# A fused attention and ELU network kernel: two plain token blocks in place of three, with all sums of weights made in the second block

## The chip, the cores and the metric

The kernel runs on one core of one Trainium2 chip. The metric is the device time of one execution in microseconds (us); lower is better. Several executions are timed and their median is used. One more execution is taken with the hardware profiler, and the profile describes that one. Five engines work side by side, each on its own queue of instructions in order: TensorE (PE, with its weight loads as PEld), VectorE (DVE), ScalarE (ACT), GpSimd (POOL), and SyncE (SP), which here issues every DMA.

## The reference

Attention runs within chunks of 64 tokens, for 8 batches of 576 tokens, 8 heads of 64 values. Its output, 4608 tokens of 512 values, goes through a two-layer network with an ELU between the layers. All arithmetic is to float32 accuracy.

```
scores = scale * matmul(q_c, k_c^T)            # q, k, v cut into chunks of 64 tokens
attn = exp(scores - max) ; attn = attn / (sum(attn) + 1e-09)
x = matmul(attn, v_c) -> [4608, 512]
h = x @ w_in                                   # w_in [512, 2048]
g = where(h > 0, h, exp(min(h, 0)) - 1)
out = g @ w_out                                # w_out [2048, 512]
```

## The kernel before

**Accuracy by parts.** TensorE multiplies in a format with fewer bits than float32 (F32R). Each operand is therefore split into a high part (`hi`, a rounded copy made on ACT) and a low part (`lo`, the difference, made on DVE or POOL), and each product is three matmuls: hi·hi, hi·lo and lo·hi (`three`, L427).

**Blocks.** The 4608 tokens are 9 blocks (`NB`) of 512 (`TB`). The 2048 hidden columns are 16 groups (`NF`) of 128, written f. A block is four tiles (`tt`) of 128 tokens; tile n of attention is made one block ahead of its use, in about ten small steps that a generator hands out (`later_attention`, L347). The steps that matter here are: two DVE transposes of q and k (L358), the score matmuls (L364), maximum and subtraction (L371, L372), exponent (L376), the sum, its reciprocal and the multiplication (L379 to L387), eight small DMAs `y<-y` that move the quarters (L396), a DVE transpose to `turned` (L398), the matmuls with v (L405), and the copy to `xf` (L410).

**Plain blocks.** The first `PLAIN` = 3 blocks take each f in turn: `hidden(f)` is 12 matmuls of 512 columns into PSUM, `elu` is two ACT steps, a DVE step (L450), the high part on ACT (L455) and the low part on DVE (L458), and `project(f)` is again 12 matmuls, one f later. The strings `FIRST_BLOCK`, `SECOND_BLOCK`, `LATER` and `LAST_STEPS` write out the order within an f: `H` is `hidden`, each `e` one step of `elu`, `P` the projection, `a` a step of the tile in work, `n` a step of the one after it.

**Blocks by seven products.** The other six blocks take two f at a time (a pair). The first layer of a pair is a 2 by 2 block product made with seven products instead of eight (a Winograd form), each 6 matmuls of 256 columns. These use sums and differences of the weight blocks: S1, S2, S3, S4, beside A11, A12, A22. They also use sums of the tokens' blocks: T1 to T4, beside B11, B21, B22, made by `prepare_x` (L581) with `x` items. `PAIRS`, `FIRST_PAIR`, `OPENING_PAIR` and `LAST_PAIR` write out the order: `p1` to `p7` are products, `c` and `d` take their results from PSUM on ACT (L632) and DVE (L637), `A` and `B` are steps of the two ELU halves, `Q` is three matmuls of 512 columns of the second layer, `w` loads a quarter of a pair's weights, `L` loads the next tile's q and k.

**Sums of weights.** `combine` (L501) makes the sums for the eight pairs g once. For each g, POOL adds high and low parts (two wide additions) and forms S1, S2, S4, S3 (four narrow ones) into one of two of the three staging buffers `kept_st`. `split(g)` cuts the sums into high and low parts, on ACT (L533) and DVE (L534). `write_parts` and `write_sums` write everything to a scratch tensor in DRAM (`a_dram`) with six DMAs (L528, L529, L539). The sums of the pair after next can start only when the writes from the same buffer have landed. One step of `combine` is issued after each f of blocks 1 and 2, three steps for each g, 27 in all. `load_operands` (L556) then reads `a_dram` back, four DMAs of 448 KB for a pair, into memory that held the plain weights.

**Tokens.** `load_tokens` (L236) reads q and k of a tile, 4 DMAs each; where a tile straddles two batches (n = 4, 13, 22, 31) it takes 8 each. Tiles up to 9 use the staging buffers 2 and 1 in turn, and later ones buffer 0, or 0 and 1.

**Queues.** PE, ACT, DVE and SP run in the order in which the program issues (`manual_schedule`). An instruction that waits holds all behind it on its engine. On SP a DMA that waits for its data holds every later DMA.

Of the kernel before, what the change touches and what calls it, by code (L numbers as in the profile page):

```python
# [10 lines left out]
F32 = mybir.dt.float32  # L11
# [4 lines left out]
ALU = mybir.AluOpType  # L16
# [4 lines left out]
def kernel(  # L21
# [35 lines left out]
    PLAIN = 3  # L57
# [289 lines left out]
    def later_attention(tt: int, qk, v_sb):  # L347
# [30 lines left out]
        z = sm.tile([P, 2, NK, 2], F32, name="z")[:, :, :, :1]  # L378
        nc.vector.tensor_reduce(out=z, in_=scores, axis=AX.X, op=ALU.add)  # L379
        nc.vector.tensor_scalar_add(z, z, 1e-9)  # L380
        nc.vector.reciprocal(z, z)
# [87 lines left out]
    def store(blk: int, o_ps, tts):  # L469
        for tt in tts:  # L470
# [6 lines left out]
            (nc.vector.tensor_copy if tt % 2 else nc.scalar.copy)(out=o, in_=o_ps[tt])  # L477
# [23 lines left out]
    def combine():  # L501
# [5 lines left out]
        def place_of(g):  # L507
            return kept_st[1 + g % 2][:, :2 * 8 * P].rearrange("p (l a f) -> p l a f", l=2, f=P)
# [33 lines left out]
        for step in range(3 * NG + 3):  # L542
            for g in range(NG):
                since = step - 3 * g - 2 + (g % 4 == 3)
                if since == 0:
                    sums(g)
                if since == 1:
                    write_parts(g, 0)
                if since == 2:
                    split(g)  # L550
                    write_parts(g, 1)
                if since == 3:
                    write_sums(g)
            yield
# [26 lines left out]
    def prepare_x(pool, tag):  # L581
# [10 lines left out]
        def part(name):  # L592
            if name in sources:
                hi, lo = b_operand(name)
                nc.scalar.copy(out=hi, in_=sources[name])
                nc.gpsimd.tensor_tensor(  # L596
# [74 lines left out]
    def warm(n: int):  # L671
# [48 lines left out]

    PAIRS = (
        "p1 c1 x1 Q p2 d1 w B Q p6 c2 B Q B x2 p5 w x3 n n Q p7 c3 d2 A w a Q Q p4 c4 A w Q p3 d3 "
        "A A Q B",
        "n a a L p1 c1 Q p2 d1 w B Q p6 c2 B Q B n n p5 w Q n p7 c3 d2 A w n l Q Q p4 c4 A w Q p3 d3 "
# [5 lines left out]
        "n a a L p1 c1 xB11 Q p2 d1 w B Q p6 c2 B Q B xB21 n p5 w xt1b n xt2b Q p7 c3 xT2 d2 A "  # L730
        "n n l Q Q p4 c4 A w Q p3 d3 A A xt4b xt3b xT1 Q w"
    )
    OPENING_PAIR = (
        "p1 c1 B Q p2 d1 xT3 B w Q p6 B c2 B Q n p5 xT4 w Q p7 c3 d2 xB22 A n w a Q Q p4 c4 A w "
# [6 lines left out]
    )  # L741
    FIRST_PAIR = (
        "Q Q Q p1 c1 xT1 xt3b Q p2 d1 xT3 Q p6 c2 xT4 w n n Q p5 xB22 w Q p7 c3 d2 w Q a A p4 c4 w "
        "p3 A d3 A A B"
# [86 lines left out]
    def place_of_tokens(n: int):  # L831

        if n < 2 * NTT + 2:
            return kept_st[2 - n % 2]
# [177 lines left out]
```

## Time and profile before

| | |
|---|---|
| timed executions | 862.87, 866.29, 864.86 us, median 864.86 us |
| the profiled execution's own time | 865.55 us |
| its span, first to last instruction | 863.8 us |
| mean granted TensorE clock | 0.996 |
| busy: ACT, DVE, POOL | 56%, 59%, 25% of the span |
| DMA moved | 180.47 MB, mean 209 GB/s |

The profile gives for each group of instructions a source line, the engine, the tile written and those read, the count, the busy time and the mean duration, and what ended the idle time before them. The chain of work that ended last goes back from the last instruction to whatever released it. The timeline lists instructions by start time, in us from the start of the span. Block 1 begins at about 134 us, block 2 at 229 us, the first pair at 320 us, and each later block is 90 us long.

### The profile page before, as it was taken

The numbers are of one execution on the slowest core, as the hardware profiler recorded it, in microseconds if no ns is written. First come the engines' busy times: TensorE is split into PE (matmuls) and PEld (weight loads), VectorE is DVE, ScalarE is ACT, GpSimd is POOL, SyncE is SP. The second block draws the span as 40 slices with busy tenths as digits, with TensorE's granted clock in tenths as the row PEclk, the third lists the DMA queues.
The fourth block names the chain that finished last, engine by engine and source line by source line (L and its number), as shares of the span: only waits on it lengthen the run. The fifth ranks groups of instructions, "written<-read, shape, count | busy, mean of one in ns | idle before, by whom it ended". The sixth has DMA issues, their size and how long they took to land.

```text
span 863.8 us, 17307 instructions
## 1 busy us (share of the span) xinstructions
PE 848.0 (98%) x6622; PEld 731.1 (85%) x6622; DVE 512.2 (59%) x841; ACT 483.7 (56%) x931; POOL 219.2 (25%) x185
## 2 busy tenths in 40 slices
PE   7899999999999999999999999999999999999998
PEld 6688887788888888888888888888888898889897
DVE  5899886556756566456644674458456854542222
ACT  5799985344544346455644565456554654465443
POOL 2000003126233023223422342234222522252221
PEclk9899999999999999999999999999999999999999
DMA  8886552546477758887778968886868798557521
GB/s 189 212 269 182 196 136 72 159 124 211 147 222 224 224 171 245 262 247 215 223 245 263 282 206 258 261 257 202 273 209 262 212 286 263 205 191 241 171 87 49
DMA packets 156707, 180.47 MB, mean 209 GB/s; under 512 B 67024, under 2 KB 123344, under 8 KB 156624
## 3 DMA queue, kind: packets, MB, share of 16 engines
q1 hardware_dynamic: 156624, 179.36, 68.0%
q8 instruction: 52, 0.85, 0.4%
q14 instruction: 31, 0.25, 0.1%
HBM read 147.85 MB, written 24.12 MB: 199 GB/s over the span
## 4 chain that ended last, share of the span: by engine, by line
PE 91%; SPq 3%; DMA 3%; DVE 2%; POOL 0%; ACT 0%; issue 0%; DVEq 0%
PE o L430 44%; PE h L430 42%; PE ps_a L364 2%; PE ps_a L405 2%; SPq L219 1%; SPq L230 1%; DMA wi_hi<-a_dram 1%; DMA k_sb<-in_k_dram 1%; DMA st<-in_moe_w_out_dram 1%; DMA y<-y 1%; PE ps_a L297 0%; PE ps_a L313 0%; SPq L396 0%; DVE glo L458 0%; PE ps_a L266 0%
## 5 line engine op out<-in xcount | busy, mean ns | idle before, releaser
L653 POOL TENSOR_TENSOR wi_lo<-e,wi_hi 128x512 fp32r<-128x512 f32 x84 | 108.6, 1293 | 325.3 <-ACT wi_hi L649 325.3
L430 PE MATMUL h<-xhi,wi_hi 128*128 128x256 f32 (+1 forms) x704 | 189.5, 315 | 0.4 <-DVE kept L637 0.3
L637 DVE TENSOR_TENSOR kept<-h,kept 128x256 f32<-128x256 f32 x144 | 60.8, 422 | 173.4 <-PE h L430 110.9
L632 ACT COPY kept<-h 128x256 f32<-128x256 f32 x192 | 70.2, 366 | 161.5 <-PE h L430 161.5
L430 PE MATMUL o<-wo_lo,wi_hi 128*128 128x512 f32 x384 | 152.3, 397 | 0.0
L430 PE MATMUL o<-wo_hi,wi_hi 128*128 128x512 f32 x384 | 152.0, 396 | 0.0
L430 PE MATMUL o<-wo_hi,wi_lo 128*128 128x512 f32 x384 | 149.4, 389 | 0.0
L430 PE MATMUL h<-xlo,wi_hi 128*128 128x256 f32 (+1 forms) x448 | 147.0, 328 | 0.1
L430 PEld LDWEIGHTS h<-xhi,wi_hi 128*128 128x128 f32 x704 | 123.4, 188 | 16.4 <-DVE kept L637 1.3
L430 PE MATMUL h<-xhi,wi_lo 128*128 128x256 f32 (+1 forms) x448 | 131.4, 330 | 0.0
L430 PEld LDWEIGHTS h<-xlo,wi_hi 128*128 128x128 f32 x448 | 84.2, 188 | 12.1 <-POOL xlo L596 0.3
L430 PEld LDWEIGHTS h<-wi_lo,wi_hi 128*128 128x128 f32 x576 | 81.6, 189 | 9.4 <-ACT kept L632 1.2
L430 PEld LDWEIGHTS h<-xhi,wi_lo 128*128 128x128 f32 x448 | 79.7, 188 | 11.2 <-DVE kept L637 0.4
L644 DVE SCALAR_TENSOR_TENSOR e<-e,kept 128x512 f32<-128x512 f32 x96 | 67.2, 700 | 34.7 <-ACT e L642 19.0
L430 PEld LDWEIGHTS o<-wo_hi,wi_lo 128*128 128x128 f32 x384 | 72.2, 188 | 16.1
L430 PE MATMUL h<-wi_lo,wi_hi 128*128 128x256 f32 x576 | 84.7, 283 | 0.0
L649 ACT CAST wi_hi<-e 128x512 fp32r<-128x512 f32 x96 | 59.8, 623 | 36.2 <-DVE e L644 35.9
L641 ACT ACTIVATE e<-kept 128x512 f32<-128x512 f32 x96 | 60.6, 632 | 34.1 <-DVE kept L637 33.7
L430 PE MATMUL o<-wo_hi,ghi 128*128 128x512 f32 x192 | 76.3, 397 | 0.0
L505 POOL TENSOR_TENSOR kept<-wi_hi,wi_lo 128x512 f32<-128x512 f32 x16 | 20.8, 1322 | 215.7 <-DVE qT L358 136.7
L430 PEld LDWEIGHTS o<-wo_lo,wi_hi 128*128 128x128 f32 x384 | 73.5, 191 | 2.3
L430 PE MATMUL o<-wo_hi,glo 128*128 128x512 f32 x192 | 74.9, 390 | 0.3 <-DVE glo L458 0.3
(98 smaller groups left out, 1382.9 us busy)
## 6 DMA issues: line engine op xcount, KB each, us to landing
wi_hi<-a_dram SPq DMA_DIRECT2D x128, 448.0 KB, 5.7
wi_lo<-a_dram SPq DMA_DIRECT2D x64, 448.0 KB, 5.7
kept<-in_q_dram SPq DMA_DIRECT2D x100, 128.0 KB, 7.4
kept<-in_k_dram SPq DMA_DIRECT2D x100, 128.0 KB, 4.4
st<-in_moe_w_in_dram SPq DMA_DIRECT2D x16, 512.0 KB, 4.2
st<-in_moe_w_out_dram SPq DMA_DIRECT2D x16, 512.0 KB, 4.8
a_dram<-kept SPq DMA_DIRECT2D x16, 512.0 KB, 4.4
y<-y SPq DMA_DIRECT2D x224, 32.0 KB, 1.9
```

The lines of the kernel that those rows point to most:

```text
L219: nc.sync.dma_start(out=dst[p0:p0 + n], in_=src[b, :, s0:s0 + n, :].rearrange("h s d -> s h d"))
L230: nc.sync.dma_start(out=v_sb[j * C:(j + 1) * C, :, c, :], in_=v[b, j::2, ss, :].rearrange("h s d -> s h d"),)
L364: nc.tensor.matmul(scores[halves[c], j, hp, :], lhsT=qT[halves[j], hp, halves[c]], rhs=kT[halves[j], hp, halves[c]], start=True, stop=True,)
L405: nc.tensor.matmul(x_ps[halves[j], c, hp, :], lhsT=v_sb[halves[c], 2 * hp + j, :], rhs=turned[halves[c], j * NK + hp, :], start=True, stop ...
L430: nc.tensor.matmul(ps, lhsT=a, rhs=b, start=start, stop=stop, skip_group_check=onto)
L505: nc.gpsimd.tensor_tensor(out=out, in0=a, in1=b, op=op)
L632: nc.scalar.copy(out=out, in_=self.x)
L637: nc.vector.tensor_tensor(out=out, in0=self.y, in1=self.kept[kept], op=ALU.add)
L641: nc.scalar.activation(out=e, in_=c, func=AF.Relu, scale=-1.0)
L644: nc.vector.scalar_tensor_tensor(out=e, in0=e, scalar=-1.0, in1=c, op0=ALU.add, op1=ALU.max)
L649: nc.scalar.copy(out=ghi, in_=e)
L653: engine.tensor_tensor(out=glo, in0=e, in1=ghi.bitcast(F32), op=ALU.subtract)
```

## The change

- `PLAIN` is 2: block 2 is now done by seven products, and block 1 is the last plain block.
- `combine` runs within block 1, in 17 steps: one at its start and one after each f. For pair g the POOL sums are issued at step `begin[g]`, and the split and all six writes at `end[g]` (the last pair's writes one step later). The two staging buffers are now 2 and 1 instead of 1 and 2.
- Tiles from 9 on use buffer 0, and odd ones above 12 buffer 2. The pair stage keeps its own results in buffer 1 instead of 2.
- In block 1, `plain_loads` issues two quarters after each of f = 9, 10, 11 and two after f = 15; before, it was 1, 2, 1 after f = 9, 10, 11 and 2, 2 after 13, 14.
- The last three plain steps and the first pair are reordered: the transposes of the following tile come one f earlier, some token sums come later, the last two ELU steps of f = 15 move behind product p2 of the first pair, products p2 and p6 follow closely, and the low part of B22 is made on DVE (`yB22`).
- In all pairs, `L` moves from the head of each second pair to the later part of each first pair. In the last pair of a block, `xt4b` moves from behind `d3` to before it.
- In attention the sum and its increment `z` are in a free part of the PSUM bank instead of SBUF; the reciprocal still goes to SBUF.
- The four results of block 0 are copied out of PSUM on ACT alone; before, two on ACT and two on DVE.

```diff
-    PLAIN = 3
+    PLAIN = 2
...
-        z = sm.tile([P, 2, NK, 2], F32, name="z")[:, :, :, :1]
-        nc.vector.tensor_reduce(out=z, in_=scores, axis=AX.X, op=ALU.add)
-        nc.vector.tensor_scalar_add(z, z, 1e-9)
-        nc.vector.reciprocal(z, z)
+        z = sm.tile([P, 2, NK, 1], F32, name="z")
+        z_ps = banks[0][:, :, NK * C:NK * C + NK].rearrange("p j (h e) -> p j h e", e=1)
+        nc.vector.tensor_reduce(out=z_ps, in_=scores, axis=AX.X, op=ALU.add)
+        nc.vector.tensor_scalar_add(z_ps, z_ps, 1e-9)
+        nc.vector.reciprocal(z, z_ps)
...
-            (nc.vector.tensor_copy if tt % 2 else nc.scalar.copy)(out=o, in_=o_ps[tt])
+            (nc.vector.tensor_copy if tt % 2 and blk else nc.scalar.copy)(out=o, in_=o_ps[tt])
...
-            return kept_st[1 + g % 2][:, :2 * 8 * P].rearrange("p (l a f) -> p l a f", l=2, f=P)
+            return kept_st[2 - g % 2][:, :2 * 8 * P].rearrange("p (l a f) -> p l a f", l=2, f=P)
...
-        for step in range(3 * NG + 3):
+        begin, end = (0, 1, 2, 4, 5, 6, 8, 9), (2, 4, 5, 6, 8, 9, 10, 12)
+        for step in range(NF + 1):
             for g in range(NG):
-                since = step - 3 * g - 2 + (g % 4 == 3)
-                if since == 0:
+                if step == end[g]:
+                    split(g)
+
+                if step == (end[g] if g < NG - 1 else end[g] + 1):
+                    write_parts(g, 0)
+                    write_parts(g, 1)
+                    write_sums(g)
+                if step == begin[g]:
                     sums(g)
-                if since == 1:
-                    write_parts(g, 0)
-                if since == 2:
-                    split(g)
-                    write_parts(g, 1)
-                if since == 3:
-                    write_sums(g)
             yield
...
     PAIRS = (
-        "p1 c1 x1 Q p2 d1 w B Q p6 c2 B Q B x2 p5 w x3 n n Q p7 c3 d2 A w a Q Q p4 c4 A w Q p3 d3 "
+        "p1 c1 x1 Q p2 d1 w B Q p6 c2 B Q B x2 p5 w x3 n n Q p7 c3 d2 A w a Q Q L p4 c4 A w Q p3 d3 "
         "A A Q B",
-        "n a a L p1 c1 Q p2 d1 w B Q p6 c2 B Q B n n p5 w Q n p7 c3 d2 A w n l Q Q p4 c4 A w Q p3 d3 "
+        "n a a p1 c1 Q p2 d1 w B Q p6 c2 B Q B n n p5 w Q n p7 c3 d2 A w n l Q Q p4 c4 A w Q p3 d3 "
         "A A Q B w",
     )
...
     LAST_PAIR = (
-        "n a a L p1 c1 xB11 Q p2 d1 w B Q p6 c2 B Q B xB21 n p5 w xt1b n xt2b Q p7 c3 xT2 d2 A "
-        "n n l Q Q p4 c4 A w Q p3 d3 A A xt4b xt3b xT1 Q w"
+        "n a a p1 c1 xB11 Q p2 d1 w B Q p6 c2 B Q B xB21 n p5 w xt1b n xt2b Q p7 c3 xT2 d2 A "
+        "n n l Q Q p4 c4 A xt4b w Q p3 d3 A A xt3b xT1 Q w"
     )
     OPENING_PAIR = (
-        "p1 c1 B Q p2 d1 xT3 B w Q p6 B c2 B Q n p5 xT4 w Q p7 c3 d2 xB22 A n w a Q Q p4 c4 A w "
+        "p1 c1 B Q p2 d1 xT3 B w Q p6 B c2 B Q n p5 xT4 w Q p7 c3 d2 xB22 A n w a Q Q L p4 c4 A w "
         "Q p3 d3 A A Q B"
     )
     LAST_STEPS = (
-        "H e e e e a xt1a xt2a xt4a xt3a P",
-        "n n H e e e P n a a e n",
-        "H xB11 n xt1b xB21 e n xt2b e n xT2 e e xt4b R",
+        "H e e e e n n a xt1a xt2a xt4a xt3a P",
+        "H e e e P n a a e xt1b xt2b",
+        "H n xB11 xB21 n e xT2 n e n R",
     )
     FIRST_PAIR = (
-        "Q Q Q p1 c1 xT1 xt3b Q p2 d1 xT3 Q p6 c2 xT4 w n n Q p5 xB22 w Q p7 c3 d2 w Q a A p4 c4 w "
-        "p3 A d3 A A B"
+        "Q Q Q p1 c1 Q p2 e e d1 xt3b xT1 p6 xT3 c2 Q xt4b Q w p5 n n xT4 yB22 Q p7 c3 d2 w Q a A p4 c4 w "
+        "p3 A d3 A A w L B"
     )
...
-        for _ in range({LOADED + 1: 1, LOADED + 2: 2, LOADED + 3: 1, NF - 3: 2, NF - 2: 2}.get(f, 0)):
+        for _ in range({LOADED + 1: 2, LOADED + 2: 2, LOADED + 3: 2, NF - 1: 2}.get(f, 0)):
             next(loading)
...
-        if n < 2 * NTT + 2:
-            return kept_st[2 - n % 2]
-        return kept_st[1 if n % 2 and n > (PLAIN + 1) * NTT else 0]
+        if n == 2 * NTT:
+            return kept_st[2]
+        return kept_st[2 if n % 2 and n > (PLAIN + 1) * NTT else 0]
...
+            if (blk, f) == (PLAIN - 1, 0):
+                next(combining)
...
-                if blk > 0:
-                    next(combining, None)
                 if blk == PLAIN - 1:
+                    next(combining)
                     plain_loads(f)
```

More of the change, by code (lines that the diff above doesn't have):

```diff
@@ L590, in prepare_x, with part @@
                        "t3": (t3, b22, b12)}
-        def part(name):
+        def part(name, engine=nc.gpsimd):
             if name in sources:
@@ L595, in part @@
                 nc.scalar.copy(out=hi, in_=sources[name])
-                nc.gpsimd.tensor_tensor(
+                engine.tensor_tensor(
                     out=lo, in0=sources[name], in1=hi.bitcast(F32), op=ALU.subtract)
@@ L883 @@
                                             for _ in range(3)][::-1]
-                                sums = kept_st[2]
+                                sums = kept_st[1]
                                 loaded = later_loads(2 * NTT)
@@ L943 @@
                         pair.add(int(item[1]))
+                    elif item == "e":
+                        acts[blk - 1, NF - 1] = next(act)
                     elif item == "A":
@@ L961 @@
                         next(following, None)
+                    elif item[0] == "y":
+                        preparing(item[1:], nc.vector)
                     elif item[0] == "x":
```

## The prediction

> **What bounds the kernel now.** The page comes first: who is busy, and for what share of the span.
>
> ```profile
> PE 848.0 (98%) x6622; PEld 731.1 (85%) x6622; DVE 512.2 (59%) x841; ACT 483.7 (56%) x931; POOL 219.2 (25%) x185
> ```
>
> PE is the bound; the others matter only where PE waits for them. The view of stretches says the same for each stage (columns: stretch, its length, busy time and count of PE, PEld, DVE, ACT, POOL, then granted clock, DMA share, GB/s).
>
> ```profile
> 153.70:246.00 92.30, 92.30 (x641) 75.80 (x641) 56.60 (x84) 42.19 (x68) 24.99 (x25) 1.00 0.55 167
> 506.77:596.77 90.00, 89.98 (x785) 79.72 (x785) 53.35 (x93) 48.95 (x97) 27.38 (x22) 1.00 0.81 248
> ```
>
> The clock is granted in full, so a stage costs its matmuls plus the waits. The chain in order of time gives periods: the same matmul, one or four tiles later.
>
> ```profile
> 172.98 2.72 PE o L430 x12
> 176.79 2.95 PE h L430 x12
> 269.11 2.95 PE h L430 x12
> 397.87 0.91 PE h L430 x6
> 420.75 0.91 PE h L430 x6
> 602.07 0.91 PE h L430 x6
> 624.44 0.91 PE h L430 x6
> ```
>
> A plain block takes 269.11 - 176.79 = 92.32 us. Within a block by seven products a tile takes 624.44 - 602.07 = 22.37 us, and across a block's end 420.75 - 397.87 = 22.88 us: each boundary holds a wait of 0.51 us, and a block takes 3 x 22.37 + 22.88 = 89.99 us. Last, the timeline of PE shows the other waits after block 0.
>
> ```profile
> 152.98 0.69 PE L405 MATMUL ps_a<-turned,v_sb 64*64 64x64 f32 x32 [0.93 <-DVE turned L398]
> ...
> 322.22 0.40 PE L430 MATMUL o<-wo_hi,ghi 128*128 128x512 f32 x1
> 322.45 0.40 PE L430 MATMUL o<-wo_lo,ghi 128*128 128x512 f32 x1
> 323.17 0.50 PE L430 MATMUL o<-wo_hi,glo 128*128 128x512 f32 x1 [0.32 <-DVE glo L458]
> ...
> 325.36 0.35 PE L430 MATMUL h<-xhi,wi_hi 128*128 128x256 f32 x1 [0.29 <-DVE kept L637]
> ...
> 443.51 0.69 PE L405 MATMUL ps_a<-turned,v_sb 64*64 64x64 f32 x32 [0.85 <-DVE turned L398]
> ```
>
> Undisturbed, one follows the last in 0.23 us (322.22 to 322.45), so from 322.45 to 323.17 PE lost 0.49, which is the bracket's 0.32 and 0.17 for the restart. With the same restart the wait at 325.36 lost 0.46, and with a smaller one at 329 us the transition to the first pair loses about 1.2 us. The two waits for `turned` lost 1.1 and 1.0 us. All that can be won beside the block itself is thus 1.1 + 1.2 + 1.0 + 5 x 0.51 = 5.9 us.
>
> **The change part by part.**
>
> *One block more by seven products:* 89.99 - 92.32 = **-2.3 us**. It also adds a sixth boundary, which is in the 89.99.
>
> *Boundaries.* DVE is what is late there:
>
> ```profile
> 406.57 1.09 DVE L380 TENSOR_SCALAR z<-z 128x8 f32<-128x8 f32 x1
> 410.59 1.54 DVE L601 TENSOR_TENSOR t<-xf,t 128x256 f32<-128x256 f32 x1
> 412.05 0.41 DVE L601 TENSOR_TENSOR t<-xf 128x256 f32<-128x256 f32 x1
> 412.38 0.41 DVE L637 TENSOR_TENSOR kept<-h,kept 128x256 f32<-128x256 f32 x1
> 185.26 0.17 DVE L380 TENSOR_SCALAR z<-z 128x8 f32<-128x8 f32 x1
> ```
>
> `d1` of the new block (412.38) ends at 412.79, and PE waits for it. Ahead of it stand the increment of z, 1.09 us where it takes 0.17 elsewhere, and two token sums of 1.54 and 0.41 (0.41 seems to be the undisturbed price). With z in PSUM and `xt4b` ahead of `d3`, up to 0.9 + 1.1 us leave this queue, and 0.17 to 0.5 are needed. But `d3` itself moves behind `xt4b`, and p2 of the next block needs it. Bounds: 0 to -0.51 for each of six boundaries; I take half: **-1.5 us**.
>
> [...]
>
> *`L` earlier.* The wait at 443.51 comes from SP:
>
> ```profile
> 420.70 7.68 SPq L247 DMA_DIRECT2D kept<-in_q_dram  x8
> 434.81 6.57 SPq L396 DMA_DIRECT2D y<-y  x8
> ```
>
> Tile 22 straddles two batches, and its 16 DMAs hold SP from 420.70 on for most of the time until 434.81, where `y<-y` comes. `L` now stands two products and some Q earlier (3 to 4 us), so `y<-y` can go some 4 us sooner, against 1.0 us needed: **-1.0 us** (0 to -1.0). In tiles with 8 DMAs nothing was late, so nothing is won.
>
> *The first wait (153 us).* ACT takes two copies from DVE, which stood between the subtraction and the sum of tile 8:
>
> ```profile
> 142.19 1.28 DVE L477 COPY q_sb<-o 128x512 f32<-128x512 f32 x2
> ```
>
> Most of the 1.28 us lay beside the exponent on ACT, on which the sum waits too. I take a quarter for `y<-y` and the PE wait behind it: **-0.3 us** (0 to -1.1).
>
> *All sums in block 1.* POOL's work is the same, in half the time; the issue is the order on ACT and DVE. `split(3)` is issued after f = 5, directly ahead of the transposes of tile 10, whose scores PE wants at 175.63; `split(6)` stands likewise ahead of tile 11, wanted at 198.71.
>
> ```profile
> 158.81 0.62 ACT L455 CAST ghi<-e 128x512 fp32r<-128x512 f32 x1 [0.75 <-DVE e L450]
> 168.55 0.98 SPq L539 DMA_DIRECT2D a_dram<-kept  x2
> 172.46 2.56 POOL L505 TENSOR_TENSOR kept<-wi_hi,wi_lo 128x512 f32<-128x512 f32 x2 [18.54 <-DMA a_dram<-kept]
> 175.10 3.38 POOL L505 TENSOR_TENSOR kept<-kept 128x256 f32<-128x256 f32 x4
> L533 ACT CAST kept<-kept 128x1024 fp32r<-128x1024 f32 x8 | 8.4, 1048 | 0.0
> L534 DVE TENSOR_TENSOR kept<-kept 128x1024 fp32r<-128x1024 f32 x8 | 11.3, 1416 | 1.2 <-ACT kept L533 1.1
> 172.38 1.08 DVE L358 STREAM_TRANSPOSE k_apart<-kept 128x512 f32<-128x512 f32 x1
> 175.63 0.69 PE L364 MATMUL ps_a<-k_apart,qT 64*64 64x64 f32 x32
> 183.40 1.22 DVE L534 TENSOR_TENSOR kept<-kept 128x1024 fp32r<-128x1024 f32 x1 [0.26 <-ACT kept L533]
> 198.71 0.69 PE L364 MATMUL ps_a<-k_apart,qT 64*64 64x64 f32 x32
> ```
>
> On the clock of the profile before: f = 3 leaves ACT at 159.43; split(1) takes ACT to 160.5 and DVE to 161.9; two writes are issued by 163.0; they land 2.9 us later, as at 169.53 to 172.46; POOL works 6.0 us (172.46 to 178.48) and ends sums(3) at 171.9; split(3) takes ACT to 173.0, DVE to 174.4, and the two transposes (1.08 each, a little overlapped: 2.0) to 176.4. With 0.1 us for the hand-over PE waits 0.9 us. From split(4), which ends where 183.40 + 1.22 stood, the same sum for tile 11 gives 199.2, a wait of 0.5 us. All that is queued behind on DVE, the ELU of f = 6 and 10, has a projection's time (2.72 us, the row at 172.98) before PE asks for it. In both places DVE's low parts and splits now run beside POOL, each up to one POOL instruction (1.3 us) later; I add 0.55 each: **+2.5 us**. Bounds: 0 if POOL ends 1 us sooner, and +8 if POOL costs 1.3 and the writes land 2.8 us later than at 172.46.
>
> The other splits stand in front of work with slack. On SP the six writes (3 us) stand ahead of `y<-y` in three tiles, whose `turned` came 4 us before its use in block 2.
>
> *The transition.* In the new order p2 and p6 follow closely, the last ELU has 1.4 us more, and `d1` is done before p5; the waits of 0.49 and 0.46 go. New: p6 needs T2's low part, made by POOL after the high part (about 0.4 us late), and p3 needs B22's low part and `d2`, which now stand behind transposes and copies (0.6 us; both are estimates from the durations shown: two transposes 2.0, a copy of 0.64). Then two quarters of the second pair's weights are issued only after f = 15, behind eight `y<-y`:
>
> ```profile
> 321.49 4.95 SPq L396 DMA_DIRECT2D y<-y  x8
> 331.36 0.39 PE L430 MATMUL h<-xhi,wi_lo 128*128 128x256 f32 x1
> wi_hi<-a_dram SPq DMA_DIRECT2D x128, 448.0 KB, 5.7
> ```
>
> With the multiplications 0.7 us later, they are issued at 327.2 and land at 332.9 by the median, 1.7 us after the second pair's first product; one that lands as soon as the writes above (3.9 us after its issue, 168.55 to 172.46) would be in time. I take 0.5. Together -1.2 + 1.0 + 0.5 = **+0.3 us** (-1.2 to +3).
>
> *Nothing:* the PLAIN tests, buffers and stores. Buffer 1 must be written out before the first pair's `c1`; that is 10 us earlier. Block 0 and the last block are unchanged.
>
> Sum: -2.3 - 1.5 - 1.0 - 0.3 + 2.5 + 0.3 = **-2.3 us** on the profiled execution's 865.55 us (span 863.8), thus 863.3. That execution lies 0.7 us above the median of 864.86; on the median's scale: **862.6 us**. A measurement of this kernel tells about 0.5%, 4.3 us, from no change: the forecast is "within".
>
> **The rivals.**
>
> *The sums hide.* If POOL ends a microsecond sooner, the +2.5 goes: -4.8. If the boundaries too give their whole 3.1 us and the transition its 1.2, it is -7.9. For it: POOL is busy only 25.0 of 92.3 us in block 1 now, and the waits found are below 1 us. Against it: two separate chains must both gain. Time: 857 to 860. Chance 0.29.
>
> *The writes land late* (slower). All of `a_dram` is written within some 70 us; the q1 traffic of block 1 rises from 167 GB/s by about half of 14.7 MB and eight loads of 448 KB, 11 MB in 92 us, to some 285 GB/s, above the 248 of the stage with a DMA share of 0.81. Each microsecond of late landing after 172.46's 2.9 moves tile 10, tile 11 and the second pair's load: 3 us for one. From 2.2 us on (a landing of 5.1 us) the time is over 4.3 us above the old one; at 3 us it is 871.6. Against it: SP issues a pair's writes in bursts with pauses of 6 us and more. Chance 0.08.
>
> *The reorderings reach nothing:* boundaries, `y<-y` and transition stay as they are, only the block and the new waits count: -2.3 + 2.5, 865. The increment of z and `xt4b` speak against it; that both wait for POOL's instructions, whose times also move, speaks for it. Chance 0.13.
>
> *POOL in the way:* low part and split, in both chains, each wait as long as the sum at 410.59 (1.54 against 0.41, 1.1 us): 4.5 us in place of my 1.1, so 866.0. For it: POOL is then busy 8 x 6.0 of 92 us in block 1. Against it: in both chains the split itself comes when the next sums still wait for their buffer. Chance 0.10. [...]
>
> **How the numbers follow.** Forecast 0.40, reorderings reach nothing 0.13, POOL in the way 0.10, sums hide 0.29, late writes 0.08. Faster by over 0.5% (below 860.5): 0.29. Within: 0.40 + 0.13 + 0.10 = 0.63. Slower: 0.08. The range from 858.5 to 866.5 leaves out the late writes and the lower third of the hidden sums.
>
> **What would show it.** Right: the period of a late block falls from 89.99 towards 89.5; no wait for `turned` near tile 21; in block 1 waits of 0.5 to 2 us at L364 for DVE's transposes, in tiles 10 and 11, with ACT's split waiting for POOL. Wrong: waits of several us in block 1 or none at all; POOL's sums held by landings of 5 us; a wait at the second pair's p1 for a load. A whole block's cost other than 90 us would upset the first term.

## The result, and the profile after

The changed kernel takes 870.2 us (median of 8 executions, 866.67 to 872.56) against 865.73 us of the kernel before on the same chip (8 executions): a ratio of 1.0055, 95% interval 1.0041 to 1.0069. On a second chip it was 869.82 against 864.01 us, 1.0070 (1.0057 to 1.0082). The forecast was 862.6 us, range 858.5 to 866.5: the kernel is slower by a little over the 0.5% that can be told, and outside the range. The profiled execution after took 869.94 us (span 868.2, mean clock 0.994), 4.4 us more than the one before.

The page's first part, of the changed kernel (lines are one to three higher than before, L364 is the same):

```profile
PE 844.5 (97%) x6766; PEld 736.4 (85%) x6766; DVE 513.8 (59%) x854; ACT 496.5 (57%) x968; POOL 245.9 (28%) x205
```

PE works 3.5 us less than before and the kernel takes 4.4 us more: the time went into waits. The timeline of PE after the first block shows them, the idle time and its releaser in brackets.

```profile
135.86 0.50 PE L431 MATMUL h<-xlo,wi_hi 128*128 128x512 f32 x1 [0.80 <-DVE xlo L424]
...
177.98 0.69 PE L364 MATMUL ps_a<-k_apart,qT 64*64 64x64 f32 x32 [1.75 <-DVE k_apart L358]
...
202.57 0.69 PE L364 MATMUL ps_a<-k_apart,qT 64*64 64x64 f32 x32 [1.45 <-DVE k_apart L358]
...
243.92 0.73 PE L406 MATMUL ps_a<-turned,v_sb 64*64 64x64 f32 x32 [2.13 <-DVE turned L399]
...
245.96 0.79 PE L431 MATMUL h<-xhi,wi_lo 128*128 128x256 f32 x2 [0.59 <-DMA wi_lo<-a_dram]
...
449.65 0.56 PE L406 MATMUL ps_a<-turned,v_sb 64*64 64x64 f32 x22 [1.13 <-DVE turned L399]
```

The waits of before at 153 us (`turned` of tile 8) and at each block's end are gone. New are one at the seam of blocks 0 and 1, the two foreseen ones for the scores of tiles 10 and 11, and a long one at the transition to the first pair, where 2.13 us for `turned` of tile 12 is followed by 0.59 us for the second pair's weights. The view of stretches (columns as in the prediction) shows that the transition cost more than these waits:

```profile
240.00:243.00 3.00, 1.79 (x41) 1.46 (x40) 0.73 (x2) 1.52 (x3) 0.00 (x0) 1.00 0.44 60
243.00:246.00 3.00, 1.50 (x35) 1.10 (x35) 1.62 (x3) 1.50 (x3) 0.84 (x1) 0.74 0.83 234
246.00:249.00 3.00, 3.00 (x12) 2.90 (x13) 0.45 (x2) 1.12 (x3) 0.43 (x1) 0.50 1.01 392
249.00:252.00 3.00, 3.00 (x14) 2.62 (x14) 1.87 (x3) 0.95 (x3) 0.00 (x0) 0.62 1.05 418
252.00:255.00 3.00, 3.00 (x21) 2.65 (x20) 1.64 (x5) 0.85 (x3) 1.30 (x1) 1.00 1.06 342
...
255.22:344.72 89.50, 89.50 (x786) 79.83 (x785) 52.83 (x93) 48.84 (x98) 27.38 (x21) 1.00 0.82 245
```

From 244 to 252 us the granted clock is 0.50 to 0.74: PE is busy, and does 12 and 14 matmuls in 3 us where it does 21 afterwards. The last row is the good part: the first block by seven products takes 89.50 us with PE busy all through.

What made `turned` late stands on SP's queue and on DVE (each row the start, the time of issue, and the count):

```profile
215.83 5.06 SPq L397 DMA_DIRECT2D y<-y  x8
...
225.01 5.38 SPq L247 DMA_DIRECT2D kept<-in_q_dram  x8
230.43 3.70 SPq L247 DMA_DIRECT2D kept<-in_k_dram  x8
234.23 1.36 SPq L219 DMA_DIRECT2D v_sb<-in_v_dram  x2
235.69 5.02 SPq L397 DMA_DIRECT2D y<-y  x8
240.75 1.68 SPq L566 DMA_DIRECT2D wi_lo<-a_dram  x2
```

```profile
212.66 0.76 DVE L388 TENSOR_TENSOR y<-ps_a,z 128x256 f32<-128x256 f32 x2
...
232.72 0.74 DVE L388 TENSOR_TENSOR y<-ps_a,z 128x256 f32<-128x256 f32 x2
...
243.15 0.71 DVE L399 STREAM_TRANSPOSE turned<-y 128x512 f32<-128x512 f32 x1 [2.42 <-DMA y<-y]
```

The data of `y<-y` is ready at 233.46 (232.72 + 0.74), but SP is still issuing the 16 token DMAs of tile 13 and the loads of v, and begins `y<-y` at 235.69, 2.2 us later. PE's wait is 2.1 us. The two quarter loads of the second pair come behind it. SP was as late one tile earlier: the data of tile 11 is ready at 213.42 (212.66 + 0.76), and its `y<-y` starts at 215.83, 2.4 us later. Between the starts of the two `y<-y` SP has 19.9 us of work, with gaps of 0.1 us at most, and the two data times are 20.0 us apart, so it cannot catch up.

The seam's wait is one that the prediction did not have. POOL forms the second pair's sums already in block 0, because its staging buffer is no longer used by tile 9:

```profile
131.97 3.28 POOL L507 TENSOR_TENSOR kept<-kept 128x256 f32<-128x256 f32 x4
...
134.59 1.22 DVE L424 TENSOR_TENSOR xlo<-xf,xhi 128x512 fp32r<-128x512 f32 x1
```

Beside it the last `glo` of block 0 took 1.15 us on DVE and the first `xlo` 1.22 us, where in the kernel before `glo` took 0.69 us and the four `xlo` took 2.49 together (start to end, one on the heels of the other):

```profile
133.41 2.49 DVE L423 TENSOR_TENSOR xlo<-xf,xhi 128x512 fp32r<-128x512 f32 x4
```

Put together, with 0.17 us for each restart of PE as in the prediction, from the two profiled executions:

| step | predicted, us | measured, us | from |
|---|---|---|---|
| start to block 1 (unchanged code) | 0 | +0.7 | the same matmul at 134.68 and 133.96 |
| seam of blocks 0 and 1 | not seen | +1.0 | 0.80 + 0.17 |
| first wait | -0.3 | -1.1 | gone |
| tiles 10 and 11 | +2.5 | +3.5 | 1.75 + 1.45 + 2 x 0.17 |
| transition | +0.3 | +5.4 | what is left of 4.4; worked out below |
| `L` earlier | -1.0 | +0.3 | 1.13 for 0.85 |
| block in place of a plain one, with its boundary | -2.3 | -2.8 | 89.50 - 92.32 |
| the five boundaries there were | -1.5 (with the sixth) | -2.5 | 5 x 0.51 gone |
| sum (of the unrounded values) | -2.3 | +4.4 | |

The transition by itself: 2.13 and 0.59 with their restarts, 0.7 us of small waits at 234 and 238 us, and (from an experiment below) some 2.6 us of the lowered clock make 6.4 us; the remainder gives 5.4 + the 1.2 of before = 6.6.

### The profile page after: what moved, and what is told of

It is laid out like the page before. It is cut to its first block, busy times and chain, and to the rows that moved or that the text cites. A ratio compares the mean times of both kernels' runs of the same rounds, so it can differ in the third digit from the quotient of the medians.

```text
span 868.2 us, 17806 instructions
## 1 busy us (share of the span) xinstructions
PE 844.5 (97%) x6766; PEld 736.4 (85%) x6766; DVE 513.8 (59%) x854; ACT 496.5 (57%) x968; POOL 245.9 (28%) x205
## 4 chain that ended last, share of the span: by engine, by line
PE 86%; DMA 4%; SPq 4%; DVE 2%; POOL 1%; ACT 1%; issue 1%; DVEq 0%; POOLq 0%; ACTq 0%
PE o L431 42%; PE h L431 39%; PE ps_a L364 2%; POOL kept L507 1%; PE ps_a L406 1%; DMA wi_lo<-a_dram 1%; SPq L219 1%; SPq L397 1%; SPq L230 1%; DMA k_sb<-in_k_dram 1%; DMA st<-in_moe_w_out_dram 1%; DMA a_dram<-kept 1%; PE ps_a L313 0%; DMA y<-y 0%; DVE kept L536 0%
## 5 line engine op out<-in xcount | busy, mean ns | idle before, releaser
L655 POOL TENSOR_TENSOR wi_lo<-e,wi_hi 128x512 fp32r<-128x512 f32 x98 | 126.6, 1292 | 387.2 <-ACT wi_hi L651 387.2
L431 PE MATMUL o<-wo_lo,wi_hi 128*128 128x512 f32 x448 | 178.0, 397 | 0.0
L431 PE MATMUL o<-wo_hi,wi_hi 128*128 128x512 f32 x448 | 177.7, 397 | 0.0
L431 PE MATMUL o<-wo_hi,wi_lo 128*128 128x512 f32 x448 | 174.5, 390 | 0.0
L431 PE MATMUL h<-xlo,wi_hi 128*128 128x256 f32 (+1 forms) x424 | 133.8, 316 | 0.8 <-DVE xlo L424 0.8
L431 PE MATMUL h<-xhi,wi_lo 128*128 128x256 f32 (+1 forms) x432 | 118.8, 319 | 0.6 <-DMA wi_lo<-a_dram 0.6
L431 PEld LDWEIGHTS h<-wi_lo,wi_hi 128*128 128x128 f32 x666 | 94.4, 189 | 10.4 <-POOL wi_lo L598 0.8
L431 PE MATMUL h<-wi_lo,wi_hi 128*128 128x256 f32 x666 | 97.7, 282 | 0.2 <-POOL wi_lo L598 0.2
L431 PEld LDWEIGHTS o<-wo_hi,wi_hi 128*128 128x128 f32 x448 | 84.8, 189 | 3.0
L644 ACT ACTIVATE e<-e 128x512 f32<-128x512 f32 x112 | 70.8, 632 | 3.6
```

The costliest lines, as they stand in the source:

```text
L431: nc.tensor.matmul(ps, lhsT=a, rhs=b, start=start, stop=stop, skip_group_check=onto)
L644: nc.scalar.activation(out=e, in_=e, func=AF.Exp, scale=-1.0)
L655: engine.tensor_tensor(out=glo, in0=e, in1=ghi.bitcast(F32), op=ALU.subtract)
```

## The experiments

**Is it SP's queue?** The theory: SP has more to issue in block 1 than it has time for, so `y<-y` waits its turn. The first test takes work from SP in block 1: the writes of the weights' own parts, 4 DMAs a pair, move into block 0. Their bytes move with them.

```diff
             for g in range(NG):
+                if step == 0 and g < NG - 1:
+                    write_parts(g, 0)
+                    write_parts(g, 1)
+                    yield
+            for g in range(NG):
                 if step == end[g]:
                     split(g)
...
-                    write_parts(g, 0)
-                    write_parts(g, 1)
+                    if g == NG - 1:
+                        write_parts(g, 0)
+                        write_parts(g, 1)
                     write_sums(g)
...
+                if blk == 0 and f > NF - NG:
+                    next(combining)
```

> The changed kernel, with the writes of the weights' own parts (4 DMAs for a pair, 7 of 8 pairs) issued on SP in the last seven steps of block 0 in place of block 1. SP gets some 2.2 us x 7 back in block 1. Theory A (the loss at the transition is SP's queue: y<-y of tile 12 is issued 2.7 us after its data is ready, behind the loads of tile 13 and the writes): y<-y is issued 2 us or more earlier, the wait of 2.1 us for turned at 243.9 and the one for the second pair's weights at 246 vanish, and the lowered clock with them; 3 to 5 us faster (865 to 867). Rival B (the DMA engines are full, not SP's queue): the same bytes move, y<-y lands no earlier, 0 to 1 us. Rival C: block 0 pays for the writes (its loads come late), and the kernel is no faster.

Measured: 863.57 against 863.82 us, 0.9997 (0.9986 to 1.0008): 5 to 6 us better than the changed kernel. PE's timeline, SP's queue and the stretches of this kernel:

```profile
176.61 0.59 PE L364 MATMUL ps_a<-k_apart,qT 64*64 64x64 f32 x25 [2.21 <-DVE k_apart L358]
...
244.26 0.74 PE L431 MATMUL h<-wi_lo 128*128 128x256 f32 x4 [0.20 <-DMA wi_lo<-a_dram]
```

```profile
230.76 1.35 SPq L219 DMA_DIRECT2D v_sb<-in_v_dram  x2
232.21 5.01 SPq L397 DMA_DIRECT2D y<-y  x8
```

```profile
178.00:180.00 2.00, 2.00 (x5) 1.56 (x6) 1.80 (x3) 0.45 (x2) 2.00 (x2) 0.50 0.85 243
```

At the transition, where 2.13 us stood, nothing is left for `turned`, and 0.20 for the weights. `y<-y` goes out at 232.21, 3.5 us earlier than in the changed kernel (235.69), and the clock stays at 1.00. That is theory A. The same matmuls, from the first of the first pair to one twelve groups behind x of tile 12, take 24.30 us in the changed kernel (231.64 to 255.94) and 19.41 here (230.34 to 249.75): 4.9 us are gained at the transition itself. They were not gained between the last two `y<-y`, where SP still has 20.4 us of work (211.81 to 232.21), the 16 token DMAs among it. SP came to tile 11 in time: it had nothing to issue from 210.34 to 211.81, where in the changed kernel it was 2.4 us late. What the test took away is the backlog from before. The test does not tell apart SP's issuing and full DMA engines: from 135 to 228 us these moved 252 GB/s in the changed kernel and 200 here. Two side results: the wait at the seam is gone too (there POOL's sums, all but one instruction, run from 136.34 us on, after `xlo`), and the wait of tile 10 grew to 2.21 us and brought a half clock with it there.

The second test moves only the two splits that stand ahead of the transposes of tiles 10 and 11 (`K` is a step of `combine`).

```diff
     LATER = (
...
-        "n n H e e e e P",
+        "n n K H e e e e P",
...
+                    elif item == "K":
+                        next(combining)
...
                 if blk == PLAIN - 1:
-                    next(combining)
+                    if f not in (5, 9):
+                        next(combining)
```

> The changed kernel, with the steps of the combination that stood after f = 5 and f = 9 (split of pairs 3 and 6, their writes, the next sums) issued after the two transposes of tiles 10 and 11, in f = 6 and 10. Theory A (the two waits for score matmuls at 178 and 202.6 come from the split's place ahead of the transposes on DVE, the split itself waiting for POOL): both waits vanish, 3.5 us less, 866.7, provided nothing else is late. Rival B (DVE is slow beside POOL whatever the order): half of the waits or more stays, 868.5 or above. Rival C (SP is full, and the writes issued later push the transition): the 3.5 us come back at 244.

Measured: 1.0064 (1.0049 to 1.0079), as slow as the changed kernel. Both score waits are gone, as theory A had it, and their time is back at 224 to 246 us, as rival C had it:

```profile
224.56 0.69 PE L406 MATMUL ps_a<-turned,v_sb 64*64 64x64 f32 x32 [1.47 <-DVE turned L399]
...
233.92 0.58 PE L431 MATMUL h<-xhi,wi_hi 128*128 128x256 f32 x1 [2.27 <-DVE e L451]
...
245.47 0.69 PE L406 MATMUL ps_a<-turned,v_sb 64*64 64x64 f32 x32 [1.80 <-DVE turned L399]
```

```profile
236.79 5.01 SPq L397 DMA_DIRECT2D y<-y  x8
```

`y<-y` of tile 12 now starts at 236.79, 1.1 us later than in the changed kernel, though PE came sooner. So the two waits were covered by a longer one: SP's queue sets the pace of block 1, and what PE gains ahead of it is lost behind it.

If so, the two edits together must give what each has, with no give-back. A first run also put tile 9's tokens back into the second staging buffer; there the second pair's sums are issued ahead of tile 9's transposes and take their place, so that tile 9 is computed from other data with the same instructions.

```diff
-        if n == 2 * NTT:
-            return kept_st[2]
+        if n < 2 * NTT + 2:
+            return kept_st[2 - n % 2]
```

> The early writes of the parts and the late splits together, and tile 9's tokens again in the second buffer, so that the second pair's sums cannot start before the end of block 0. Theory A (three separate losses of the changed kernel, at 135.9 about 1 us, at 178 and 202.6 3.5 us, at the transition some 5 us): 9 to 10 us faster than the changed kernel, 860.5 to 861.5, and 4 to 5 faster than the kernel before. Rival B (one shared limit, DMA or POOL): less than 5 us, 865.5 or above.

Measured: 861.19 against 863.82 us, 0.9976 (0.9963 to 0.9989). The second run leaves tile 9 alone and has the two edits only:

> The early writes of the parts and the late splits together, nothing else; every tile's tokens in their own buffer. Theory A (two separate causes, the order on DVE in tiles 10 and 11 and SP's queue at the transition): the score waits at 176.6 (2.4 us) and the lowered clock behind them (1 us or more) go, and as SP now has room, they do not come back at the transition; 3 to 4 us faster than with the early writes alone: 0.996 of the kernel before, and 0.990 to 0.991 of the changed kernel. Rival B (one shared limit): what goes at 177 comes back at 225 to 245, as with the late splits alone; the same time as with the early writes alone, 1.000.

Measured: 861.67 against 864.01 us, 0.9973 (0.9962 to 0.9984), and 0.9906 of the changed kernel on the same chip (861.67 / 869.82). Theory A again: no wait at L364 is left, and at the transition SP keeps up:

```profile
227.54 1.36 SPq L219 DMA_DIRECT2D v_sb<-in_v_dram  x2
229.00 5.00 SPq L397 DMA_DIRECT2D y<-y  x8
```

```profile
233.41 0.86 PE L431 MATMUL h<-wi_lo,wi_hi 128*128 128x256 f32 x5 [0.25 <-POOL wi_lo L604]
...
260.30 0.51 PE L406 MATMUL ps_a<-turned,v_sb 64*64 64x64 f32 x19 [0.76 <-DVE turned L399]
```

This is a version faster than both kernels. The third test of the queue was meant to gain more: the last two quarter loads of the second pair from behind f = 15 to behind f = 12, and tile 22's tokens half a tile earlier.

```diff
-        for _ in range({LOADED + 1: 2, LOADED + 2: 2, LOADED + 3: 2, NF - 1: 2}.get(f, 0)):
+        for _ in range({LOADED + 1: 2, LOADED + 2: 2, LOADED + 3: 2, LOADED + 4: 2}.get(f, 0)):
...
-        "n n l Q Q p4 c4 A xt4b w Q p3 d3 A A xt3b xT1 Q w"
+        "n E n l Q Q p4 c4 A xt4b w Q p3 d3 A A xt3b xT1 Q w"
...
+                    elif item == "E":
+                        if n + 2 == 22:
+                            ahead = load_tokens(22 * P, place_of_tokens(22))
...
+                        if n + 1 == 22:
+                            loaded = ahead
```

> The same two, and two steps more. The two quarter loads of the second pair, which the change put behind f = 15, stand behind f = 12; and the 16 token DMAs of tile 22 are issued half a tile earlier, ahead of y<-y of tile 20, where SP waited for it with nothing to issue. Theory A: SP's order makes both waits; the one for the second pair's weights at the transition (0.5 to 1.5 us) and the one for turned near 443 us (1.1 to 1.3 us) go; 2 us faster than the run before it, 0.994 of the kernel before. Rival B (the DMA engines move the bytes no faster, and y<-y lands late in whatever order): the waits stay, no faster than the run before it.

Measured: 866.48 against 864.01 us, 1.0029 (1.0019 to 1.0040), 4.8 us slower than without these two steps. A miss, and the most telling one:

```profile
219.39 2.37 SPq L572 DMA_DIRECT2D wi_lo<-a_dram  x2
221.81 6.89 SPq L247 DMA_DIRECT2D kept<-in_q_dram  x8
228.74 3.71 SPq L247 DMA_DIRECT2D kept<-in_k_dram  x8
...
233.99 5.86 SPq L397 DMA_DIRECT2D y<-y  x8
```

```profile
242.30 0.60 PE L406 MATMUL ps_a<-turned,v_sb 64*64 64x64 f32 x12 [4.42 <-DVE turned L399]
```

```profile
240.00:243.00 3.00, 0.70 (x25) 0.70 (x28) 1.47 (x3) 0.14 (x1) 0.00 (x0) 0.50 0.73 221
```

Two DMAs put ahead of tile 13's tokens move `y<-y` from 229.00 to 233.99. Issuing them takes 2.37 us, where it took 1.05 us for the same two behind `y<-y`. PE then waits 4.42 us, and the matmuls of the transition take 25.26 us (227.37 to 252.63), where in the repaired kernel they take 19.10 (227.01 to 246.11). The wait near 440 us is gone in this run, and one of 1.44 us for a weight load is new at 425 us, so that the 4.8 us are those of both steps. Theory A is right in its cause and was wrong in its forecast: of the two places tried for these loads, the one behind f = 15, which the change chose, is the better.

**Why does the clock fall?** The changed kernel was timed and profiled again as a measure:

> The changed kernel unchanged, timed on the same chip as the other runs of this set, as their measure. Expected 1.0055 of the kernel before, as the first time (0.5% slower), with the granted clock falling near 245 us in the profile if PE again waits over 2 us there.

Measured: 1.0070 (1.0057 to 1.0082). In this execution tile 10's wait was a little longer than in the first profile (1.82 for 1.75 us), and here the clock fell behind it too:

```profile
177.82 0.59 PE L364 MATMUL ps_a<-k_apart,qT 64*64 64x64 f32 x25 [1.82 <-DVE k_apart L358]
...
245.14 1.13 PE L406 MATMUL ps_a<-turned,v_sb 64*64 64x64 f32 x32 [3.11 <-DVE turned L399]
```

```profile
178.00:180.00 2.00, 2.00 (x67) 1.73 (x63) 1.23 (x3) 1.21 (x2) 1.92 (x2) 0.83 1.14 390
180.00:182.00 2.00, 2.00 (x6) 1.58 (x5) 1.05 (x2) 0.58 (x1) 1.92 (x4) 0.50 1.00 394
182.00:184.00 2.00, 2.00 (x8) 1.60 (x8) 0.00 (x0) 0.45 (x1) 2.00 (x3) 0.82 1.10 255
```

To test cause and price, PE was given work during the wait: matmuls into a half of the bank that x of tile 12 overwrites afterwards. It adds work and takes none away. First, repeated score matmuls in the changed kernel:

```diff
-    def later_attention(tt: int, qk, v_sb):
+    def later_attention(tt: int, qk, v_sb, again=0):
...
+        for _ in range(again):
+            for hp in range(NK):
+                for j, c in quarters:
+                    nc.tensor.matmul(
+                        banks[0][halves[c], j, NK * C + hp * C:NK * C + (hp + 1) * C],
+                        lhsT=qT[halves[j], hp, halves[c]],
+                        rhs=kT[halves[j], hp, halves[c]], start=True, stop=True,
+                    )
...
-        return later_attention(n % NTT, qk, v_sb)
+        return later_attention(n % NTT, qk, v_sb, 4 if n == 13 else 0)
```

> The changed kernel, with the score matmuls of tile 13 issued four times more into the half of the bank that x of tile 12 overwrites afterwards, so that PE works (some 2 us) while it would have waited for turned of tile 12. Nothing waits for them but PE. Theory A (the fall of the granted clock to 0.5 to 0.74 in 243 to 252 us follows PE's idle stretch of 2.1 us): the clock stays at 1.00 there, the x matmuls come at the same time, and the kernel is 2 to 2.5 us faster than the changed one (867.5 to 868.2 on the scale of 870.2). Rival B (the fall has another cause, such as the heat of block 1): the clock falls all the same, no change (870.2 +- 0.5).

Measured: the clock stayed at 1.00 after the transition and the profiled execution took 867.82 us, 2.1 less than that of the changed kernel; but the six timed executions spread from 867.72 to 873.77 us, 1.0073 (1.0047 to 1.0098), which does not tell it from the changed kernel. The same filling, eightfold, in the kernel with the 4.42 us wait:

> The kernel of the run with both further steps (second pair's quarters behind f = 12, tile 22's tokens half a tile earlier), in which PE stood idle for 4.4 us at 242 us and the granted clock fell to 0.5 for 8 us; here the score matmuls of tile 13 are issued eight times more into a half of the bank that is overwritten afterwards, so that PE is busy in those 4.4 us. Theory A (idle PE for over 1.8 us makes the clock fall): turned comes at the same time, the clock stays at 1.00, and the kernel is 2.5 to 4 us faster than without the filling: 0.9985 to 1.000 of the kernel before in place of 1.0029. Rival B (the clock falls for another reason, or PE was idle because it was throttled): 1.003, and the clock falls as before.

Measured: 1.0043 (1.0030 to 1.0057), slower than without it, against theory A; yet the clock stayed at 1.00 from 60 us to the end of its profiled execution. There `turned` came 1.2 us later counted from the same matmul at 83 to 86 us, and the start up to that matmul took 3.1 us longer than in the run without filling (85.94 for 82.87 us), at a lower clock (0.50 to 0.90 in the five rows of 4 us from 16 to 28 and from 36 to 44 us; without the filling only two rows of the first 60 us lie below 1.00, 0.59 and 0.99). Whether the 256 instructions themselves cause this is open. So the filling was made small: 18 wide matmuls, in the changed kernel.

```diff
+        for i in range(again):
+            w = w_out_slices(0)[0]
+            nc.tensor.matmul(banks[0][:, i % 2, NK * C:], lhsT=w[:, :P], rhs=w[:, :NK * C],
+                             start=True, stop=True)
...
+        return later_attention(n % NTT, qk, v_sb, 18 if n == 13 else 0)
```

> The changed kernel with 18 matmuls of 128x256 (0.12 us each from start to start, 2.1 us together) behind the score matmuls of tile 13, on weights that are there, into the half of the bank that x of tile 12 overwrites: the same filling as in the first run, with 18 instructions in place of 128, so that little else moves. Theory A (PE idle for more than some 1.8 us makes the granted clock fall): turned comes as late as before, PE's idle stretch before x of tile 12 shrinks from 2.1 to 3.1 us to at most 1.1 us, the clock stays at 1.00 from 240 to 256 us, and the matmuls behind it regain 2 us; 867.5 on the scale of 869.8, 1.0045 of the kernel before (1.0055 and 1.007 in the two runs of the changed kernel). Rival B: the clock falls without the idle stretch too; 1.0055 to 1.007.

Measured: 867.19 against 864.54 us, 1.0036 (1.0020 to 1.0051). This lies below the interval of the changed kernel's second timing (1.0057 to 1.0082) and overlaps with that of its first (1.0041 to 1.0069), so the gain on the whole kernel is likely and not settled. The trace is plainer:

```profile
240.35 0.69 PE L364 MATMUL ps_a<-k_apart,qT 64*64 64x64 f32 x32
240.98 2.41 PE L370 MATMUL ps_a<-wo_hi 128*128 128x256 f32 x18
243.32 0.69 PE L410 MATMUL ps_a<-turned,v_sb 64*64 64x64 f32 x32
```

```profile
246.00:249.00 3.00, 3.00 (x22) 2.74 (x22) 2.32 (x4) 1.30 (x5) 0.25 (x1) 1.00 1.04 409
```

x of tile 12 comes no sooner after the scores (2.97 us; 2.82 in the changed kernel), but the clock is 1.00 behind it: from x to the same matmul of the second layer, twelve groups of three or six on, it is 9.17 us (243.32 to 252.49) in place of 12.02 (243.92 to 255.94). That is 2.85 us, of which some 0.2 is the shorter wait for weights (0.42 for 0.59). Without the filling the clock fell at this place in three profiles (2.13, 3.11 and 4.42 us idle), and with it in none of three. Idle PE makes the clock fall, and by these profiles that costs more here (some 2.6 us) than the wait itself.

**The boundaries and `L`.** The kernel before, with nothing but z in PSUM (the lines of the change's diff; the reciprocal stays in SBUF):

> The kernel before, with z's sum, increment and inverse in PSUM, as the changed kernel has them, and nothing else. Theory A (the wait of 0.51 us at a block's end comes from DVE's increment of z, 1.09 us in SBUF beside POOL): the period across a boundary falls from 22.88 to 22.37 us in all five boundaries, 2.5 us less. Rival B (the order of the token sums, xt4b, is what counts): the period stays 22.88. [...]

Measured: 861.51 us in its one execution, and all tile periods 22.37 us, boundaries too. DVE's row for the increment, and a block across its boundary:

```profile
405.95 0.17 DVE L381 TENSOR_SCALAR ps_a<-ps_a 128x8 f32<-128x8 f32 x1
```

```profile
342.00:431.50 89.50, 89.50 (x786) 79.85 (x785) 52.80 (x92) 48.92 (x99) 27.39 (x21) 1.00 0.78 241
```

The increment takes 0.17 us in place of 1.09, and that alone removes all 0.51 us; `xt4b` still stands at its old place in this kernel. Timed:

> The kernel before with z in PSUM, timed (its one look showed no wait at any boundary and none at 443 us: five times 0.51 and 1.0 us). Theory A: 3 to 3.5 us faster than the kernel before, 0.996, so that z in PSUM alone is worth as much as the whole change with its damage undone, but for the block's 2.3 us. Rival B (the look was a lucky execution): 0.998 or above.

Measured: 862.57 against 864.11 us, 0.9973 (0.9962 to 0.9983); a little less than theory A's 0.996, and near the five boundaries' 2.5 us. Last, the repaired kernel with `L` back at its old place (the five strings of the change undone for this item):

> The early writes of the parts and the late splits, as before, with the item L (the token loads of the next tile) back at its old place, behind the first x copies of a tile's second pair. Theory A (putting L earlier lengthens SP's queue ahead of y<-y and wins nothing; the wait near 443 us was DVE's, and z in PSUM alone removed it in the kernel before): the waits for turned at 260.3 (0.95 us) and 439.8 (0.46 us) go, 1 to 1.4 us faster than with L at its new place: 0.9955 to 0.996 of the kernel before. Rival B (the earlier L helps y<-y, as the prediction had it): the wait near 440 us grows to 1 us or more, and the kernel is 0.5 to 1 us slower, 0.998.

Measured: 862.5 against 864.11 us, 0.9972 (0.9959 to 0.9986), the same as with the new place. The waits for `turned` stayed (0.58 us idle at 261.9 us for 0.76 at 260.3; 0.71 at 441.8 for 0.27 at 439.8), and one of 0.83 us for the second pair's weights came at 240.3. Neither theory: where `L` stands makes no difference that these runs show. What sets the wait for `turned` between 439 and 450 us, 0.17 to 1.15 us idle in the runs with two plain blocks and tile 22's tokens in their usual place, stays open.

## Why the prediction was wrong

**The step that failed is the transition, forecast at +0.3 us (-1.2 to +3) and measured at +5.4.** Its working counted the reordered instructions and two late quarter loads, and set `y<-y` to the multiplications plus a fixed lag, with SP free. (By its own rows the two loads land 1.5 us behind the second pair's first product, 332.9 - 331.36, where it wrote 1.7; that is not what failed.) It left out what SP had ahead of them. Before the change the tile loaded in those steps has 8 token DMAs; now it is tile 13, which straddles two batches and has 16, and the writes of the sums come ahead of them in the same block. The 16 alone just fit (the early writes show it); with the writes of the earlier pairs SP was already 2.4 us late at tile 11, and had no room to catch up. The prediction used exactly this fact for tile 22 (16 DMAs that hold SP), and it noted six writes ahead of `y<-y` in block 1 as covered by 4 us of slack from block 2; that slack did not exist any more. Relief of SP took the matmuls of the transition from 24.30 to 19.41 us, and two more DMAs ahead of `y<-y` took them from 19.10 to 25.26. Whether SP's issues were long because the DMA engines were full stays open. The lowered clock is part of this term: nothing of it was in the prediction, and it is nearly half of the loss (some 2.6 of 5.4 us).

**All sums in block 1**, +2.5 forecast, +3.5 measured: the mechanism and both places were right, to the split that waits for POOL:

```profile
162.03 0.95 SPq L541 DMA_DIRECT2D a_dram<-kept  x2
...
167.39 2.70 POOL L507 TENSOR_TENSOR kept<-wi_hi,wi_lo 128x512 f32<-128x512 f32 x2 [3.59 <-DMA a_dram<-kept]
170.17 3.40 POOL L507 TENSOR_TENSOR kept<-kept 128x256 f32<-128x256 f32 x4
...
173.61 1.05 ACT L535 CAST kept<-kept 128x1024 fp32r<-128x1024 f32 x1 [2.87 <-POOL kept L507]
...
174.69 1.23 DVE L536 TENSOR_TENSOR kept<-kept 128x1024 fp32r<-128x1024 f32 x1 [2.61 <-ACT kept L535]
```

POOL ends at 173.57, 1.7 us after the forecast's 171.9. The writes were issued by 162.98, as forecast (163.0), but landed 4.4 us later, at 167.39, where the sum took 2.9; that is 1.5 of the 1.7. The order does the rest. In tile 11 POOL's own sums took longer, 7.0 us for 6.0 (191.15 to 198.17). With the splits behind the transposes both waits are gone. But this term hid behind the other: removed by itself it gave nothing. **The seam**, +1.0, stood in no term: the prediction held block 0 for unchanged, though the freed buffer lets POOL start its sums there.

**Boundaries**, -1.5 forecast, -3.1 measured for six: half was taken, the whole came, from z alone, whose increment took 0.17 us in PSUM in place of 1.09; `xt4b` was not needed.

**Block by seven products**: right (89.50 with its boundary). **First wait**: all 1.1 us went, where 0.3 was taken, but the mechanism (two copies fewer on DVE) is not shown: in the kernel before with z alone the wait falls from 0.93 to 0.32 and 0.49 us idle in its two profiles. **`L` earlier**, -1.0: wrong, it gives nothing; with z alone the wait at 443 us is gone in both profiles, with `L` at its old place.

**The rivals.** The slower one, late writes (chance 0.08), gave the right sign and a stage of 255 to 318 GB/s (150 to 220 us) near its 285. The late landing that it named is there at tile 10 (4.4 us), for a small part of the loss; what decided was SP's queue. "POOL in the way" holds for the seam, which it did not name; the two splits of tiles 10 and 11 took 1.23 us each on DVE, as undisturbed (1.22 us before); "the reorderings reach nothing" falls with the boundaries. "The sums hide" is nearest to the repaired kernel's 0.9973, but needs two edits that the change lacks.

**The expected gain** of the change is there: -2.8 for the block, -2.5 for boundaries, -1.1 for the first wait, 6.4 us. It is given back in block 1 and at the transition. And z may be most of what the repaired kernel gains: the kernel before with z alone is as fast (0.9973 each, on two chips). In the profiles the repaired kernel is 1.4 to 2.4 us shorter from 83 us on; the medians do not show it.

## What to carry to other kernels

When work is moved into fewer steps, add up the issue time of each queue for the stretch, also of the queue that only issues DMAs, and put the urgent transfers (here `y<-y`) where nothing long stands ahead of them (two DMAs more ahead of it moved it from 229.00 to 233.99). A wait that a longer one covers gives nothing when it is removed alone (the late splits by themselves: 1.0064 of the kernel before), so test removals together. And a PE wait near 2 us should be priced with the slower matmuls behind it (here 2.13 us idle at 243.9, and some 2.6 us behind it at a clock of 0.50 to 0.74).

## What the runs showed of the hardware

The granted clock fell to 0.50 in or behind every idle stretch of PE in the traces from 1.82 us on, and behind none up to 1.80 us (after the first 60 us; idle time as in the brackets of the timeline; the longest stretches):

| idle, us | kernel, at us | lowest granted clock behind it |
|---|---|---|
| 1.75 | changed, 178.0 | 1.00 |
| 1.80 | 18 wide matmuls, 177.3 | 1.00 |
| 1.80 | repeated score matmuls, 178.1 | 1.00 |
| 1.80 | late splits, 245.5 | 1.00 |
| 1.82 | changed again, 177.8 | 0.50 |
| 2.13 | changed, 243.9 | 0.50 |
| 2.21 | early parts, 176.6 | 0.50 |
| 2.27 | late splits, 233.9 | 0.50 |
| 3.11 | changed again, 245.1 | 0.50 |
| 4.42 | both further steps, 242.3 | 0.50 |

Taken as 0.50 for a time and 1.00 around it, it stayed low for 3.4 us at the stretches of 1.82, 2.21 and 2.27 us (for the first from the rows of the changed kernel's second profile, 2 x (0.17 + 0.50 + 0.18) / 0.50), and by the same sum over rows of 2 or 3 us for 6.8 us, twice as long, at those of 2.13, 3.11 and 4.42 us. That idle PE is the cause is shown by the filling; that the bound is a fixed 1.8 us is not, with so few cases.

One issue of a DMA on SP has no fixed price: two quarter loads took 1.05 us behind `y<-y` in the repaired kernel and 2.37 us ahead of tile 13's tokens, and the eight q loads of tile 13 took 5.20 us with the late splits, 5.38 in the changed kernel and 6.89 with both further steps, where the eight k loads behind them took 3.70 or 3.71.
